# Retention block and SwiGLU feed-forward on one core: the first tile's key rows made on the chip instead of loaded a second time

## The chip, the core and the metric

The kernel runs on one core of a Trainium2 chip. The core has five instruction queues that matter here: TensorE (PE in the profile; its weight loads are listed as PEld), VectorE (DVE), ScalarE (ACT), GpSimd (POOL) and SyncE (SP), which only issues transfers. Each works through its own instructions in order and waits for others by semaphores; transfers (DMA) are carried out by 16 engines that all queues share. The metric is the device time of one execution in microseconds, lower is better; a value given for a kernel is the median of its runs.

## The reference

Eight sequences (batch) of 576 tokens, eight heads of 64 features. Each head has a decay; the scores of queries and keys are weighted by the decay to the power of the distance and summed over the values (no softmax). The result, laid out as 4608 tokens of 512 features, goes through a gated feed-forward layer.

```python
scores = scale * np.matmul(q, k.transpose(0, 1, 3, 2))            # (8, 8, 576, 576), scale = 1/8
gamma = 1.0 - 2.0 ** (-5.0 - np.arange(H))
Dmat = np.where(rel >= 0, gamma[:, None, None] ** rel[None], 0.0)  # rel = query position - key position
attn = np.matmul(scores * Dmat[None], v)
x = attn.transpose(0, 2, 1, 3).reshape(B * S, H * D)               # (4608, 512)
g = x @ w_gate                                                     # 512 x 1536
out = (g * (1.0 / (1.0 + np.exp(-g))) * (x @ w_val)) @ w_out       # (4608, 512), float32
```

## The kernel before

**Pairs.** Attention is done two heads at a time: 8 sequences by 4 pairs of heads make 32 pairs, numbered 0 to 31. A pair's 576 tokens are cut into nine chunks of 64. Within a chunk the scores are computed outright; what earlier chunks add comes through a running state (the decayed sum of key times value). Each pair therefore needs its keys in two layouts: by token (`kn`, tokens on partitions), which together with the values gives the states in `new_states`, and by feature (`kT`, features on partitions, 128 x 576), which together with the queries by feature (`qT`) gives the scores in `scores`.

**Loads.** `load(i)` issues the transfers of pair i, two pairs ahead of its use. Pairs 0 to 3 are special: they are loaded by token and turned by TensorE. From pair 4 on SyncE issues ten transfers a pair (for pairs 4 to 19): `kn` by token (L290, 288 KB), the values `v` by token (L290, 288 KB), then four transfers of 72 KB for the queries and four for the keys (L299). These eight write runs of 32 features, 128 bytes each, into `qk`, so that every 32x32 block of the result lies in `qk` untransposed: partition a*32 + t holds, for quarter a of the pair's features, the tokens j*32 + t. One VectorE transpose of 32x32 blocks over the whole 128 x 576 tile then gives `qT`, a second one `kT` (both L477).

**Buffers.** `qk` has two buffers (pair 11 has a place of its own in `rest`), `kn` three, `v` four; `kT` and the states have one. A load waits until the last reader of the buffer's earlier content is done.

**Ticks.** `tick(t)` advances three pairs by a step. On TensorE: own values of pair t-2 (L517), states of pair t-1 (L528), earlier values of t-2 (L540, L544), scores of t-1 (L552, L558). Behind these, as a list of pieces that are handed to the other engines in turn: ScalarE copies half of the states out of PSUM (`copies`, L569) and scales the keys by token with their decays in place (`keys`, L492), the outputs of pair t-2 go to the tile x of the feed-forward layer (VectorE, or ScalarE for pairs 8 to 19), VectorE masks the scores (L565, L575) and sums the states (L581 to L593), and at the end come the pieces that `transposes(t)` returns for pair t: for pairs 8 to 19 a scaling of the queries on ScalarE (L474), then the two transposes of L477. The next tick's scores need them.

**Tiles.** The feed-forward layer works on tiles of tokens: the first of 512, four more of 1024. The first tile is computed plainly: the up stage multiplies twelve blocks f of 128 hidden features (`up0`, L871, gate into one PSUM bank and value into another, two pairs of banks in turn), ScalarE takes the silu of the gate (L874) and VectorE multiplies it with the value (L875). Then follows the down stage (`down0`, L882). Into these two stages the ticks 4 to 13 are laid by hand: `tick_at` puts ticks 4 to 9 behind blocks f of the up stage and ticks 10 to 13 behind steps of the down stage. The later tiles use schemes with fewer products (L1208 and L1415), with sums on VectorE and GpSimd; pairs 12 to 31 are attended to there.

**Weights.** In the up stage the feed-forward weights are still on their way. `load_w` fetches a raw block (from the sixth on GpSimd issues it) into one of three places; `split` has ScalarE take the wanted bits out of it (L398, L399), and `rounding` has VectorE put them together (L415, L416). `split(j+1)` writes the buffer that `rounding(j-1)` has read, and a raw place is free for the next load when it has been split. In the list of work, silu follows splits on ScalarE, and rounding follows the transposes of the tick before on VectorE.

Of the kernel before, what the change touches and what calls it, by code (L numbers as in the profile page):

```python
# [132 lines left out]
def kernel(  # L133
# [32 lines left out]
    nc = tc.nc  # L166
# [5 lines left out]
    HP = H // 2  # L172
    L = D
    NC = S // L
    NFULL = S // P
    CW = NFULL * P
    SQ = 32
# [59 lines left out]
    def needed(n):  # L237

        last = (min(starts[n] + TW, NT) - 1) // S
        return last * HP + HP - 1 + 3  # L240
# [3 lines left out]
    def whole(i):  # L244

        return HP <= i < needed(2) - 2

    def scaled(i):

        return 0 < i < HP  # L250

    def tokens(src, b, p):
        return src[b, 2 * p : 2 * p + 2].rearrange("h t d -> (h t) d").rearrange("(g p) d -> p g d", p=P)

    def load(i):

        b, p = divmod(i, HP)
        t = kp.tile([P, NC * D], F32, tag="v", name="v", bufs=4)
        late = [rest[:, dn_at + 1280 * (i - 2) + 640 * n :][:, 0 : NC * D] for n in range(2)] if 1 < i < HP else None
        kn = late[1] if late else kp.tile([P, NC * D], F32, tag="kn", name="kn")  # L260
        queue = nc.sync
        if i < HP:
            qk = late[0] if late else ld.tile([P, 2, S // SQ, SQ], F32, tag="qk", name="qk").rearrange("p n j d -> p (n j d)")[:, 0 : NC * D]
            queues = (nc.sync, nc.scalar if i < 2 else nc.sync)
            heads = range(2 * p, 2 * p + 2)
            blocks = lambda a: a[:, 0:CW].rearrange("p (c h d) -> p h c d", h=2, d=D)
            for h, queue in zip(heads, queues):
                if scaled(i):
                    queue.dma_start(out=early[i][:, ts(h % 2, CW // 2)], in_=q[b, h, 0:CW].rearrange("(p c) d -> p (c d)", c=NFULL))
                else:  # L270
                    queue.dma_start(out=blocks(qk)[:, h % 2], in_=q[b, h, 0:CW].rearrange("(c p) d -> p c d", p=P))
            for h, queue in zip(heads, queues):
                queue.dma_start(out=blocks(kn)[:, h % 2], in_=k[b, h, 0:CW].rearrange("(c p) d -> p c d", p=P))
                if i == 0 and queue is nc.sync:
                    nc.sync.dma_start(out=tab[:, 0:NCOL], in_=decays[:, 0:NCOL])

            def values():
                for h in heads:
                    queues[i % 2].dma_start(out=blocks(t)[:, h % 2], in_=v[b, h, 0:CW].rearrange("(c p) d -> p c d", p=P))

            loaded[i] = (qk, kn, t)
            return values
        else:
            if i == needed(1) - 3:
                qk = rest[:, 4096 : 4096 + 2 * S].rearrange("p (n j d) -> p n j d", n=2, d=SQ)
            else:
                qk = ld.tile([P, 2, S // SQ, SQ], F32, tag="qk", name="qk")
            for dst, src in ((kn, k), (t, v)):
                if whole(i):
                    queue.dma_start(out=dst.rearrange("p (g d) -> p g d", d=D), in_=tokens(src, b, p))  # L290
                    continue
                for hl in range(2):
                    queue.dma_start(out=dst[:, 0:CW].rearrange("p (c h d) -> p c h d", h=2, d=D)[:, :, hl, :],
                                    in_=src[b, 2 * p + hl, 0:CW, :].rearrange("(c p) d -> p c d", p=P))
            if not whole(i):
                queue.dma_start(out=t[:, CW : CW + D], in_=v[b, 2 * p : 2 * p + 2, CW:S, :])
            for n, src in enumerate((q, k)):
                for a in range(P // SQ):
                    queue.dma_start(  # L299
                        out=qk[a * SQ : (a + 1) * SQ, n],  # L300
                        in_=src[b, 2 * p + a // 2, :, (a % 2) * SQ : (a % 2 + 1) * SQ].rearrange("(j t) d -> t j d", t=SQ))
        loaded[i] = (qk, kn, t)
# [14 lines left out]
    decays = nc.inline_tensor(table, name="decays").ap()  # L317
    NCOL = 6 * H + 4 * HP + 4 + P
    values = [load(0), load(1)]
    ident = const.tile([P, P], F32, name="ident")  # L320
    make_identity(nc, ident)
    nc.scalar.activation(out=io[:, 0:1], in_=ident[:, 0:1], func=AF.Silu)
    for f in values:
        f()
    load(2)()
    inv, key = tab[:, 0:H], tab[:, H : 2 * H]
    step = tab[:, 2 * H : 2 * H + 2 * HP]
# [25 lines left out]
    for u in range(NF // 2):  # L353
        for gv, w in enumerate((moe_w_gate, moe_w_val)):
            src = w[:, u * 2 * P : (u + 1) * 2 * P].rearrange("(c p) n -> p c n", p=P)
            weights.append((src, [w_up[:, u // 2, gv, 2 * (u % 2) + f].rearrange("p k x -> p (k x)") for f in range(2)]))
    NUP = len(weights)
    for u in range(NF // 2):
        src = moe_w_out[u * 2 * P : (u + 1) * 2 * P, :].rearrange("(f p) n -> p f n", p=P)
# [60 lines left out]
    for m in range(2):  # L420
        load_w(m, (0,))
    load(3)()
    for m in range(2):
        load_w(m, (1,))
# [3 lines left out]
    kT = const.tile([P, S], F32, name="kT")  # L428
# [22 lines left out]
    def light(i):  # L451

        return needed(1) - 6 <= i < needed(2) - 2

    def transposes(i):
        p = i % HP
        qk, kn, vt = loaded.pop(i)
        qT = early[i] if i < HP else qp.tile([P, S], F32, tag="qT", name="qT")
        st[i] = dict(qT=qT, kn=kn, v=vt)
        pieces = []  # L460

        if i < HP:

            for n, (t, src, bank) in enumerate(((kT, kn, bankC), (qT, qk, bankE))):
                for c in range(NFULL):
                    nc.tensor.transpose(bank[:, c : 4 * P : NFULL] if n else bank[:, ts(c, P)], src[:, ts(c, P)], ident)
                pieces.append(lambda t=t, bank=bank: nc.scalar.copy(t[:, 0:CW], bank))
        else:
            if light(i):
                def scale_q():  # L470

                    src = qk[:, 0].rearrange("p (j r) d -> p r j d", r=2)
                    for r in range(2):
                        nc.scalar.activation(out=src[:, r], in_=src[:, r], func=AF.Copy, scale=piece[:, 2 * p + r : 2 * p + r + 1])  # L474
                pieces.append(scale_q)
            for n, t in enumerate((qT, kT)):
                pieces.append(lambda n=n, t=t: nc.vector.transpose(out=t, in_=qk[:, n].rearrange("p j d -> p (j d)")))  # L477

        every = slice(0, P)

        def keys():
            blocks = kn.rearrange("p (g d) -> p g d", d=D)
            if whole(i):
                parts = [(0, every, blocks[:, 0:NFULL]), (1, every, blocks[:, NFULL:NC])]
            else:
                parts = [(hl, every, blocks[:, hl : 2 * NFULL : 2]) for hl in range(2)]
            for hl, rows, at in parts:
                scale = key[rows, 2 * p + hl : 2 * p + hl + 1]
                if 1 < i < HP:
                    nc.gpsimd.tensor_scalar(out=at, in0=at, scalar1=scale, scalar2=None, op0=ALU.mult)  # L490
                else:
                    nc.scalar.activation(out=at, in_=at, func=AF.Copy, scale=scale)  # L492

        if light(i):
            return [lambda: (keys(), pieces[0]())] + pieces[1:]
        return pieces + [keys] if i < HP else [keys] + pieces
# [216 lines left out]
    pieces = []  # L713

    def scale_run(i):
        if scaled(i):
            src = early[i].rearrange("p (h c d) -> p h c d", h=2, d=D)
            dst = loaded[i][0][:, 0:CW].rearrange("p (c h d) -> p h c d", h=2, d=D)
            table = run[:, 8 * i : 8 * i + 8].rearrange("p (h c) -> p h c", h=2).unsqueeze(3).to_broadcast([P, 2, NFULL, D])
            nc.gpsimd.tensor_tensor(out=dst, in0=src, in1=table, op=ALU.mult)  # L720
# [62 lines left out]
    def turn_pair(i):  # L783
        for f in transposes(i):
            f()

    def tick(t, lo=HP, hi=NP, spread=False, then=None):
# [16 lines left out]
        if lo <= t - 1 < hi and whole(t - 2) and not whole(t - 1):  # L804
            decay(slice(0, H), slice(0, H), half[1])
        copies, *masks = masked(t - 1) if lo <= t - 1 < hi else (lambda: None,)
        keys, *new = transposes(t) if lo <= t < hi else (lambda: None,)
        outputs = to_x(t - 2)[0] if lo <= t - 2 < hi else lambda: None
        late = needed(1) - 4 <= t < needed(1) - 2 or light(t - 2)
# [658 lines left out]
    earlier_values(1)  # L1468
    to_x(1)[0]()
    put = transposes(3)  # L1470
    rounding(1, False)
    for f in put:
# [164 lines left out]
```

## Time and profile before

| what | value |
|---|---|
| median of three runs | 1013.4 us (1013.31, 1013.4, 1019.88) |
| profiled execution, its own time | 1012.77 us |
| span of that execution in the profile | 1011.0 us |
| granted TensorE clock | 1.00 throughout |
| packets of SyncE's queue from 39 to 125 us | 46,086, 7.78 MB, 60.0% of the 16 engines' time |
| median time of a 72 KB key load from issue to landing, 39 to 125 us | 5.9 us |
| weight loads by GpSimd, 1024 KB, the same | 7.1 to 9.4 us |

All times inside the profile count from the start of the span. Pairs 4 to 11 are prepared between 45 and 153 us: the first tile's up stage runs until 122.4 us, its down stage until 172.8 us. The prediction shows lines of the page (busy time and share of each engine), of the windows (busy time of each engine in a stretch) and of the timeline (start, duration, engine, line, operation, output<-input with shapes, count; in brackets the time that the engine sat idle before it and who ended that).

### The profile page before, as it was taken

What the parts mean: (1) busy time and instruction counts of PE and PEld (TensorE: products, weight loads), DVE (VectorE), ACT (ScalarE), POOL (GpSimd) and SP (SyncE); (2) the same over time, 40 slices, a digit from 0 to 9 for tenths busy, and PEclk for the clock granted to TensorE, in tenths of its full rate; (3) what the DMA queues carried; (4) which work ended last, traced back from release to release, by engine and by line L of the source; (5) the groups of instructions that cost most, each with busy time, mean ns of one, the idle gap of its engine ahead of it and who ended that gap; (6) DMA issues with size and microseconds to landing.
All of it is one profiled execution on the core that took longest, in us unless ns stands there. A gap on an engine that the chain in (4) does not pass through costs nothing.

```text
span 1011.0 us, 21336 instructions
## 1 busy us (share of the span) xinstructions
PE 1002.8 (99%) x8330; PEld 827.7 (82%) x8330; DVE 717.8 (71%) x1210; ACT 285.7 (28%) x636; POOL 576.3 (57%) x611
## 2 busy tenths in 40 slices
PE   8999999999999999999999999999999999999998
PEld 7645455888888888888888888888888888888887
DVE  5568988678886676977777678866575767566745
ACT  4654622122423321133321202233320012232110
POOL 3511358979587228565565157746672586566614
PEclk9999999999999999999999999999999999999999
DMA  9999977888787886957578786434454454445553
GB/s 228 276 252 281 200 216 260 211 239 217 168 211 235 219 197 218 211 156 198 177 187 222 179 196 202 151 137 155 162 173 141 156 188 146 148 153 185 178 163 103
DMA packets 273932, 194.44 MB, mean 192 GB/s; under 512 B 212328, under 2 KB 241896, under 8 KB 273832
## 3 DMA queue, kind: packets, MB, share of 16 engines
q1 hardware_dynamic: 249448, 99.49, 40.5%
q10 hardware_dynamic: 20208, 79.57, 24.2%
q0 software_dynamic: 4176, 14.03, 4.2%
q8 instruction: 66, 1.08, 0.5%
q14 instruction: 34, 0.28, 0.1%
HBM read 154.11 MB, written 38.93 MB: 191 GB/s over the span
## 4 chain that ended last, share of the span: by engine, by line
PE 91%; SPq 3%; DMA 2%; DVE 1%; issue 1%; ACT 1%; ACTq 0%; DVEq 0%
PE bankB L1208 12%; PE bankE L1208 12%; PE bankA L1208 12%; PE bankC L1208 12%; PE bankE L1415 7%; PE bankC L1415 7%; PE bankB L1415 7%; PE bankA L1415 6%; SPq L299 2%; PE outer L1208 2%; PE inner L1208 2%; PE outer L517 2%; PE outer L544 1%; PE inner L558 1%; PE inner L528 1%
## 5 line engine op out<-in xcount | busy, mean ns | idle before, releaser
L1061 POOL TENSOR_TENSOR rest<-rest 128x512 f32<-128x512 f32 (+1 forms) x143 | 150.7, 1065 | 158.1 <-DVE rest L1061 110.3
L1223 POOL TENSOR_TENSOR arena<-rest,io 128x256 f32<-128x256 f32 x168 | 123.8, 749 | 78.7 <-ACT io L1222 78.1
L1222 ACT ACTIVATE io<-rest 128x256 f32<-128x256 f32 x192 | 79.3, 417 | 209.9 <-DVE rest L1061 139.2
L1208 PE MATMUL bankB<-rest,arena 128*128 128x256 f32 x428 | 110.1, 381 | 0.0
L1208 PE MATMUL bankE<-rest,arena 128*128 128x256 f32 x424 | 107.8, 379 | 0.0
L1061 DVE TENSOR_TENSOR rest<-bankC,rest 128x512 f32<-128x512 f32 x112 | 75.8, 684 | 40.4 <-PE bankC L1208 23.3
L1061 DVE TENSOR_TENSOR rest<-bankB,rest 128x512 f32<-128x512 f32 x110 | 74.8, 685 | 41.5 <-PE bankB L1208 30.4
L1208 PE MATMUL bankA<-rest,arena 128*128 128x256 f32 x408 | 104.0, 379 | 0.0
L1061 DVE TENSOR_TENSOR rest<-bankA,rest 128x512 f32<-128x512 f32 x112 | 75.9, 685 | 38.8 <-PE bankA L1208 20.2
L1061 DVE TENSOR_TENSOR rest<-bankE,rest 128x512 f32<-128x512 f32 x116 | 78.5, 686 | 29.2 <-PE bankE L1208 17.1
L1208 PE MATMUL bankC<-rest,arena 128*128 128x256 f32 x368 | 94.2, 380 | 0.0
L1208 PEld LDWEIGHTS bankB<-rest,arena 128*128 128x128 f32 x428 | 80.7, 190 | 11.9 <-DVE rest L1061 0.9
L1208 PEld LDWEIGHTS bankE<-rest,arena 128*128 128x128 f32 x424 | 80.5, 190 | 11.0
L1208 PEld LDWEIGHTS bankA<-rest,arena 128*128 128x128 f32 x408 | 77.5, 190 | 10.6
L1208 PEld LDWEIGHTS bankC<-rest,arena 128*128 128x128 f32 x368 | 69.4, 190 | 10.0 <-DVE rest L1061 0.6
L1061 POOL TENSOR_TENSOR arena<-arena 128x256 f32<-128x256 f32 (+1 forms) x76 | 70.6, 951 | 8.3 <-PE bankC L1208 7.0
L1415 PE MATMUL bankE<-arena 128*128 128x256 f32 x264 | 61.0, 381 | 0.0
L1415 PE MATMUL bankC<-arena 128*128 128x256 f32 x264 | 60.9, 380 | 0.0
L1415 PEld LDWEIGHTS bankE<-arena 128*128 128x128 f32 x264 | 49.8, 190 | 7.0 <-POOL arena L904 0.2
L1415 PEld LDWEIGHTS bankC<-arena 128*128 128x128 f32 x264 | 49.9, 190 | 6.9
L1415 PE MATMUL bankB<-arena 128*128 128x256 f32 x240 | 55.3, 380 | 0.0
L1415 PE MATMUL bankA<-arena 128*128 128x256 f32 x228 | 52.5, 380 | 0.0
(294 smaller groups left out, 1880.1 us busy)
## 6 DMA issues: line engine op xcount, KB each, us to landing
arena<-up ACTq DMA_DIRECT2D x60, 896.0 KB, 4.8
arena<-dn ACTq DMA_DIRECT2D x60, 384.0 KB, 3.4
arena<-dn SPq DMA_DIRECT2D x44, 384.0 KB, 4.4
out_dram<-rest SPq DMA_DIRECT2D x31, 256.0 KB, 3.5
qk<-in_q_dram SPq DMA_DIRECT2D x108, 72.0 KB, 4.1
qk<-in_k_dram SPq DMA_DIRECT2D x108, 72.0 KB, 3.8
dn<-rest SPq DMA_DIRECT2D x26, 256.0 KB, 3.1
up<-arena SPq DMA_DIRECT2D x13, 512.0 KB, 3.4
```

What stands on the lines that cost most here:

```text
L299: queue.dma_start(out=qk[a * SQ : (a + 1) * SQ, n], in_=src[b, 2 * p + a // 2, :, (a % 2) * SQ : (a % 2 + 1) * SQ].rearrange("(j t) d -> t ...
L517: m = nc.tensor.matmul(value(i, hl, c), s["v"][rows, at], ret[rows, c % 2 if whole(i) else hl, c // 2], start=start, stop=start, skip_grou ...
L528: nc.tensor.matmul(z[half[hl], r, c], s["kn"][chunk(i, hl, 2 * c + r)], s["v"][rows, at], start=True, stop=True, skip_group_check=True)
L544: nc.tensor.matmul(xr[half[hl]] if c + 1 == NC else value(i, hl, c), state[half[hl], c, :], s["qT"][half[hl], ts(c, L)], start=False, stop ...
L558: nc.tensor.matmul(sc[chunk(i, hl, 2 * c + r)[0], r if whole(i) else hl, c], kT[half[hl], at], qT[half[hl], at], start=True, stop=True, sk ...
L1061: eng.tensor_tensor(out=out, in0=a, in1=b, op=ALU.add if sign > 0 else ALU.subtract)
L1208: m = nc.tensor.matmul(b[:, g * TB : (g + 1) * TB], w[:, g], x, start=(opens and g == 0), stop=True, skip_group_check=True)
L1222: nc.scalar.activation(out=s, in_=src[:, 0:TB], func=AF.Silu)
L1223: (nc.vector if busy and o != 2 and qd + 1 < NQ else nc.gpsimd).tensor_tensor(out=hid[:, qd, 2 * H + h, 2 * T + t], in0=src[:, TB : 2 * TB ...
L1415: nc.tensor.matmul(b[:, m * TB : (m + 1) * TB], lhs[:, qd, ts(m, P)], w[:, qd], start=(opens and qd == 0 and m == 0), stop=(qd == NQ - 1), ...
```

## The change

For pairs 4 to 11, those that are turned before the second tile begins, the keys by feature are no longer loaded. VectorE transposes the 32x32 blocks of `kn` (keys by token, before they are scaled) into the half of `qk` in which the loaded keys used to stand. In that form a partition holds 32 features' worth of one of four token groups, with the two heads' and the two halves' blocks interleaved; sixteen ScalarE copies, each of 32 partitions and four or five blocks of 32 elements, put the blocks into the places that they have in `kT`. The query loads, the query transposes and all TensorE work stay. Pairs 12 to 31 keep the loads as they were.

```diff
+    def by_token(i):
+
+        return HP <= i < needed(1) - 2
+
...
-            for n, src in enumerate((q, k)):
+            for n, src in enumerate((q,) if by_token(i) else (q, k)):
                 for a in range(P // SQ):
                     queue.dma_start(
...
-            for n, t in enumerate((qT, kT)):
-                pieces.append(lambda n=n, t=t: nc.vector.transpose(out=t, in_=qk[:, n].rearrange("p j d -> p (j d)")))
+            flat = [qk[:, n].rearrange("p j d -> p (j d)") for n in range(2)]
+            pieces.append(lambda: nc.vector.transpose(out=qT, in_=flat[0]))
+
+            def rows_of_k():
+
+                blocks = flat[1].rearrange("p (g n t) -> p g n t", n=2, t=SQ)
+                to = kT.rearrange("p (c w t) -> p c w t", w=2, t=SQ)
+                for r in range(2):
+                    for hl in range(2):
+                        cs = slice((hl + r) % 2, NC, 2)
+                        gs = slice(hl * (NC // 2 + (1 - r)), hl * (NC // 2 + (1 - r)) + len(range(NC)[cs]))
+                        for w in range(2):
+                            for n in range(2):
+                                nc.scalar.copy(out=to[(2 * hl + n) * SQ : (2 * hl + n + 1) * SQ, cs, w],
+                                               in_=blocks[(2 * r + w) * SQ : (2 * r + w + 1) * SQ, gs, n])
+
+            if by_token(i):
+                nc.vector.transpose(out=flat[1], in_=kn)
+                pieces.append(rows_of_k)
+            else:
+                pieces.append(lambda: nc.vector.transpose(out=kT, in_=flat[1]))
```

`HP` is 4 and `needed(1)` is 14, so `by_token` holds for pairs 4 to 11. The transpose of `kn` is issued when `transposes(t)` is called, ahead of the tick's pieces; the copies are the last of them. In the order of the built program nothing else moves on any engine: VectorE has the same number of transposes, ScalarE has 128 instructions more, and SyncE's queue is 32 transfers shorter.

## The prediction

> **What bounds the kernel now.** I read the share of each engine first, then the windows of the first 180 us (all eight changed pairs lie there), then the places in the TensorE timeline where it sat idle, and from these back along ScalarE and VectorE.
>
> ```profile
> PE 1002.8 (99%) x8330; PEld 827.7 (82%) x8330; DVE 717.8 (71%) x1210; ACT 285.7 (28%) x636; POOL 576.3 (57%) x611
> ```
>
> ```profile
> 39.40:122.40 83.00, 81.17 (x846) 45.25 (x844) 64.09 (x130) 48.07 (x88) 21.55 (x31) 1.00 1.06 241
> 122.40:172.80 50.40, 50.31 (x577) 25.82 (x574) 44.62 (x76) 13.03 (x41) 35.23 (x28) 1.00 0.82 247
> ```
>
> TensorE is busy for 1002.8 of 1011.0 us. The first window is the first tile's up stage with the ticks of pairs 4 to 9, the second its down stage with pairs 10 and 11. After the window's borders and length come the busy us of PE, PEld, DVE, ACT and POOL, then the granted clock (1.00), the DMA share and GB/s. TensorE is idle for 83.00 - 81.17 = 1.83 us in the first window and 0.09 in the second. The DMA share of 1.06 says that the engines which move data have no slack there; ScalarE has 83.00 - 48.07 = 35 us. So nearly all that can be won lies in 1.83 us, two gaps:
>
> ```profile
> 71.47 3.70 PE L871 MATMUL bankA<-rest,arena 128*128 128x512 f32 x8 [0.52 <-ACT io L874]
> 103.74 3.70 PE L871 MATMUL bankA<-rest,arena 128*128 128x512 f32 x8 [1.30 <-ACT io L874]
> ```
>
> The bracket is the idle time before and who ended it: ScalarE's silu, which frees a bank. Why was the silu late? ScalarE works in order, and ahead of each late silu it had stood waiting to split weights (L398):
>
> ```profile
> 67.18 0.69 ACT L398 ACTIVATE rest<-rest 128x512 f32<-128x512 f32 x1 [10.23 <-DVE arena L415]
> ...
> 99.52 0.69 ACT L398 ACTIVATE rest<-rest 128x512 f32<-128x512 f32 x1 [8.51 <-issue]
> ...
> 103.11 0.58 ACT L874 ACTIVATE io<-bankA 128x512 f32<-128x512 f32 x1
> ```
>
> The split overwrites a buffer that VectorE's rounding (L415) reads, and VectorE was held by the transpose of the keys, which waited for their load:
>
> ```profile
> 65.36 0.78 DVE L477 STREAM_TRANSPOSE kT<-qk 128x576 f32<-128x576 f32 x1 [5.03 <-DMA qk<-in_k_dram]
> ...
> 97.44 0.78 DVE L477 STREAM_TRANSPOSE kT<-qk 128x576 f32<-128x576 f32 x1 [3.01 <-DMA qk<-in_k_dram]
> 98.15 0.85 DVE L710 TENSOR_TENSOR x_odd<-outer,tab 128x128 f32<-128x128 f32 x3
> 99.01 0.43 DVE L415 TENSOR_SCALAR arena<-rest 128x512 int32<-128x512 int32 x1
> ```
>
> L415 at 99.01, L398 at 99.52, so the 8.51 us called "issue" are this chain too. The last of a pair's ten loads, the keys by feature, is what holds TensorE.
>
> **What is removed.** For pairs 4 to 11, the four key loads of 72 KB each: 32 issues on SyncE. In its timeline these groups take 7.02, 5.61, 2.13, 4.32, 3.51, 3.48, 2.79 and 2.13 us, 31 us in sum, in which everything behind them in that queue stood: the next pair's loads, the second table (L1485), and from 132.0 us the operand stores (L974). At 128 bytes a packet an issue is 576 packets; the 28 issues from 39 us to 125 us are 16,128 packets. That window's DMA view has 46,086 packets of SyncE's queue taking 60.0% of 16 engines' 86 us, 17.9 ns each; so some 18 us of all engines together are freed (an estimate from that mean). TensorE gains only what ends its two gaps.
>
> Gap one: without the 5.03 us wait VectorE ends pair 5's query transpose at 60.3 us plus the 0.75 of a transpose now ahead of it, has L415 behind it at about 62, and the silu stands at 66 where it stood at 70.83; needed at 70.95. Gone with 5 us to spare. Gap two: the query transpose of pair 7 ended at 94.4 with no wait; plus 0.75, plus L710's 0.85, L415 ends at 96.5. Three splits take 99.52 to 103.11 = 3.6 us in the trace, silu 0.6: ready at 100.7, needed at 102.44 - 0.52 = 101.9. Gone by 1.2 us, if ScalarE is ready to split at 96.5. Gain 1.82 us.
>
> **What is moved.** VectorE keeps two transposes a pair, of one form (128x576, 0.73 to 0.78 us); the keys' is now issued at the head of the tick, from the key tile that was loaded as the pair's first. It therefore delays masks and outputs by 0.75 us and gives that back where the old one stood. The scaling of the keys (L492) now waits for it: at ticks 6 and 7 until 76.0 and 90.3 instead of 74.6 and 88.9, at tick 9 until 126.1 instead of 122.86. Queued behind are only the query scaling and the copies, then splits; TensorE wants tick 9's keys at 129.74 (L528): 0.86 us of scaling fits, cost nothing. The buffer of pair t's queries and keys comes free for pair t+2 when the copies end, no longer with VectorE; copies of pair 6 would end at 80.4, the old transpose ended at 80.7: nothing.
>
> **What is added.** Sixteen ScalarE copies a pair, 32 partitions by 128 or 160 elements (mean 144), SBUF to SBUF, 128 in all. No row has this form. The nearest:
>
> ```profile
> 118.36 0.62 ACT L935 ACTIVATE x_odd<-rest 128x512 f32<-128x512 f32 x1
> 118.88 0.62 ACT L935 ACTIVATE rest<-rest 128x512 f32<-128x512 f32 x1
> ...
> 133.23 0.53 ACT L611 COPY rest<-outer 64x128 f32<-64x128 f32 x2
> 133.67 0.96 ACT L492 ACTIVATE kn<-kn,tab 128x256 f32<-128x256 f32 x2
> ```
>
> L935 is SBUF to SBUF with a constant: 0.62 us long, the next starts 0.52 later. The slope from PSUM copies of 256 and 512 elements (371 and 586 ns) is 0.84 ns an element; 368 fewer make it 0.31 long and 0.21 apart. L611, 64x128 out of PSUM: 133.23 to 133.67 is two, 0.22 apart. Upper bound: L492 and L474, 256 to 320 elements with a scale from a table, 0.43 apart. I take 0.21, since size, source and constant come from the nearest rows: 3.4 us a pair, 27 us in all. Bounds 0.21 and 0.43, with 0.31 where one copy begins only when the last has ended.
>
> [...]
>
> What hides the block: 35 us of idle ScalarE in the first window against five blocks (17 us), and room up to the pair's scores. Each block starts when keys (and from pair 8 the queries) are scaled and must end when TensorE reaches L552 in the next tick:
>
> - pair 4: 46.2 to 53.8; pair 5: 55.7 to 70.0; pair 6: 77.0 to 87.7; pair 7: 91.1 to 112.4; all over 7 us
> - pair 8: 116.8 to 121.7, 4.9 us; pair 9: 127.85 to 131.05, 3.2 us; pair 10: 135.4 to 140.35, 4.95 us; pair 11: 144.7 to 153.1
>
> Pair 9 starts late because VectorE runs without idle from 97.4 us and reaches its key transpose only at 125.3. At 3.4 us only pair 9 is late, by 0.2. For gap two, pair 7's block ends at 94.5 and a split behind it at 95.7, ahead of 96.5.
>
> **Sum**, on the profiled execution (1012.77 us, span 1011.0): -0.52 - 1.30 + 0.2 = -1.6, so 1011.2. The median of the runs shown, 1013.4, is 0.6 above it: 1011.8 us. A measurement of this kernel can tell about 1% from no change, so this is no change in that sense. From 172.8 us on TensorE has no wait for these engines, so the 1.6 us should come through whole.
>
> **Rivals.**
>
> *The gain is given back.* The copies do not overlap: 16 x 0.31 = 5.0 us. Pair 8 then is 0.1 us late, pair 9 1.8, pair 10 0.05; 1.9 against 1.8: 1013.5 us. For: the copies of four ticks carry a wait on their own engine. Against: L398 carries such waits too and keeps 0.57 us between starts at 0.67 length. [...]
>
> *ScalarE sets the end, slower.* At 0.43 the block is 6.9 us and comes after its scores: pair 8 late by 2.0, pair 9 by 3.7 less these 2.0, pair 10 by 1.9, together 5.6; in gap two the split behind pair 7's block starts at 99.2, so 1.30 stays and only 0.52 is won: +5.1, 1018.5 us. It decides from 0.31 a copy on. For: two SBUF rows show 0.43. Against: both have a table operand and up to twice the elements. Over 1% slower would need copies near 0.6 us, which only 512 elements reach here.
>
> *The relief does not reach TensorE.* Splits run earlier but weights are not there: those of gap two were issued by GpSimd at 84.4 and 87.2 and such loads took 7.1 to 9.4 us, so 96.6 against 96.5. If they also are late by the whole 3 us, gap two stays: 1013.1 us. Against: fewer packets in their way.
>
> **How the numbers follow.** Forecast 0.60, given back 0.15, relief not reaching 0.12, slower 0.13. The range runs from 1009.5 (all gained, and up to 2 us between executions) to 1018.5. Faster by over 1% would need 10 us and TensorE idles 8 in all: 0.01. Slower by over 1%: 0.05 of the 0.13, if copies are dearer than any row. Within 1%: 0.94.
>
> **What would show it.** Right: no key wait in VectorE's waits, both L871 gaps under 0.1 us, the new copies 0.20 to 0.25 us apart, L552 of pairs 9 and 10 with under 0.3 us of idle time. Wrong: TensorE waiting for the copies at L552 by over 1 us, a silu still ending a gap near 102 us, or idle TensorE after 173 us.

## The result and the profile after

The changed kernel is slower by half a per cent: 1019.5 us median of 22 runs (1017.73 to 1022.61) against 1013.32 us for the kernel before, run on the same chip. The ratio is 1.0052 with a 95% interval of 1.0038 to 1.0067; that is 5.3 us (3.9 to 6.8), while the two medians lie 6.2 us apart. The forecast was 1011.8 us in a range of 1009.5 to 1018.5. The profiled execution took 1019.25 us, with a span of 1017.6 us and a granted clock of 1.00. Lines have moved in the new file: splits are L402 and L403, roundings L419 and L420, the keys' scaling L515, the transposes L497 (keys) and L481 (queries), the copies L493, states L551, scores L575, up stage L894, silu L897, product L898, down stage L905.

The page's first line after, the busy time of each engine:

```profile
PE 1005.1 (99%) x8330; PEld 828.2 (81%) x8330; DVE 715.2 (70%) x1210; ACT 324.0 (32%) x764; POOL 576.0 (57%) x611
```

ScalarE has the 128 added instructions and 38.3 us more of busy time. The windows of the first tile's up and down stage, with borders where TensorE now begins and ends them:

```profile
39.40:123.85 84.45, 82.11 (x847) 45.74 (x845) 61.77 (x129) 70.09 (x166) 18.97 (x29) 1.00 0.89 221
123.85:178.70 54.85, 51.18 (x574) 26.24 (x574) 43.92 (x77) 29.75 (x93) 39.82 (x32) 1.00 0.63 209
```

TensorE idles 2.34 us in the first (1.83 before) and 3.67 us in the second (0.09 before), while ScalarE is still idle for 14 us of the first and 25 us of the second. The DMA share fell from 1.06 and 0.82 to 0.89 and 0.63. So the transfers went and room in ScalarE was left, as the averages promised, and the time was lost all the same. The timeline of TensorE says where (idle time and its releaser in the bracket):

```profile
104.10 3.70 PE L894 MATMUL bankA<-rest,arena 128*128 128x512 f32 x8 [1.46 <-ACT io L897]
123.11 0.27 PE L575 MATMUL outer<-qT,kT 64*64 64x64 f32 x1 [0.77 <-ACT kT L493]
131.53 0.46 PE L540 MATMUL outer<-ret,v 64*64 64x64 f32 x16 [0.56 <-DVE ret_last L598]
133.56 0.69 PE L551 MATMUL inner<-v,kn 64*64 64x64 f32 x32 [1.57 <-ACT kT L493]
136.41 0.27 PE L575 MATMUL outer<-qT,kT 64*64 64x64 f32 x1 [1.27 <-ACT kT L493]
```

The gap at 71.47 us is gone. The one at 103.74 us (1.30) is still there at 104.10 us (1.46). Four new ones follow, in the ticks of pairs 9 and 10. The next table gives how late TensorE stands: the start of the same instruction after, minus before. A step can be larger than the gaps in the brackets: 1.08 against 0.77 us at the scores of pair 8, 3.99 against 0.56 + 1.57 + 1.27 = 3.40 at those of pair 9. What makes up the rest was not settled.

| at | lag, us | step |
|---|---|---|
| 46 us, ahead of the first changed pair | +0.36 | start-up, differs from run to run |
| behind the scores of pair 4 | +0.79 | +0.43 |
| behind the first gap of before | +0.20 | -0.59 |
| behind the second gap of before | +0.36 | +0.16 |
| behind the scores of pair 8 (down stage starts, 122.39 to 123.83) | +1.44 | +1.08 |
| behind the scores of pair 9 (131.71 to 137.14) | +5.43 | +3.99 |
| behind the scores of pair 10 (141.03 to 146.96) | +5.93 | +0.50 |
| end of the down stage (172.77 to 178.70) | +5.93 | 0 |

Two thirds of it is one tick, that of pair 10, in which the scores of pair 9 are computed. To see what that tick waits for, first ScalarE's timeline around it:

```profile
117.78 5.28 ACT L493 COPY kT<-qk 32x160 f32<-32x160 f32 x16
123.08 0.69 ACT L402 ACTIVATE rest<-rest 128x512 f32<-128x512 f32 x1
123.67 0.66 ACT L403 ACTIVATE rest<-rest 128x512 int32<-128x512 uint32 x1
124.22 0.60 ACT L897 ACTIVATE io<-bankC 128x512 f32<-128x512 f32 x1
...
129.35 0.96 ACT L515 ACTIVATE kn<-kn,tab 128x256 f32<-128x256 f32 x2 [3.24 <-DVE qk L497]
130.22 0.95 ACT L478 ACTIVATE qk<-qk,tab 128x288 f32<-128x288 f32 x2
131.07 5.29 ACT L493 COPY kT<-qk 32x160 f32<-32x160 f32 x16
```

A row of the timeline merges neighbours of one kind: "x16" of 5.28 us is the whole block of a pair, both sizes. VectorE's timeline in the same stretch:

```profile
124.85 0.69 DVE L898 TENSOR_TENSOR arena<-bankE,io 128x512 f32<-128x512 f32 x1 [2.97 <-ACT io L897]
125.46 1.50 DVE L419 TENSOR_SCALAR rest<-rest 128x512 int32<-128x512 int32 x1
127.00 1.64 DVE L420 CUSTOM_DVE_ANT_0 rest<-rest 128x1024 uint16<-128x1024 uint16 x1
128.56 0.77 DVE L497 STREAM_TRANSPOSE qk<-kn 128x576 f32<-128x576 f32 x1
...
132.99 0.48 DVE L616 SCALAR_TENSOR_TENSOR state<-state,tab,inner 128x256 f32<-128x256 f32 x1
```

Read the two as one chain. The copies of pair 8 hold ScalarE from 117.78 to 123.06 us. The last silu of the up stage stands behind them and starts at 124.22. Before, it started at 117.88:

```profile
117.88 0.58 ACT L874 ACTIVATE io<-bankC 128x512 f32<-128x512 f32 x1
```

After, VectorE waits 2.97 us for it with its product. Behind the product in VectorE's queue are the two roundings, and behind these pair 9's key transpose, at 128.56. Now ScalarE waits 3.24 us for that transpose, because the keys may be scaled only after it. Then come two scalings and pair 9's copies, which end at 136.36. The first two scores of pair 9 start at 134.87; the others wait for these copies and start at 136.41. So one block delays the next one by way of the other engine, once round.

VectorE's queue delays TensorE at a second place. The same stretch before, first VectorE, then TensorE:

```profile
122.21 0.68 DVE L875 TENSOR_TENSOR arena<-bankE,io 128x512 f32<-128x512 f32 x1
...
129.07 0.47 DVE L593 SCALAR_TENSOR_TENSOR state<-state,tab,inner 128x256 f32<-128x256 f32 x1
```

```profile
129.74 0.65 PE L528 MATMUL inner<-v,kn 64*64 64x64 f32 x32
```

VectorE's last sum of the states ended at 129.54 us before, and TensorE wrote the next states into the same PSUM place (`inner`) from 129.74 on: 0.2 us of slack. After, the product is 2.64 us later and the sum 3.92, since a longer rounding (1.50 us, 0.89 before) and the transpose now lie between. The sum ends at 133.47 us, and the states start at 133.56. The trace names the copies as releaser of that wait of 1.57 us; by the times it is VectorE.

The copies themselves, as groups by line and shape for the seven pairs that use `qk` (busy us, mean ns of one, idle before):

```profile
L493 ACT COPY kT<-qk 32x160 f32<-32x160 f32 x56 | 17.9, 320 | 1.0
L493 ACT COPY kT<-qk 32x128 f32<-32x128 f32 x56 | 16.5, 295 | 1.2
```

One is 0.31 us long on average, and the block of sixteen takes 5.1 to 5.3 us, 0.32 to 0.33 us from start to start: they don't overlap at all.

### The profile page after: what moved, and what is told of

It is laid out like the page before. It is cut to its first block, busy times and chain, and to the rows that moved or that the text cites. A ratio compares the mean times of both kernels' runs of the same rounds, so it can differ in the third digit from the quotient of the medians.

```text
span 1017.6 us, 21435 instructions
## 1 busy us (share of the span) xinstructions
PE 1005.1 (99%) x8330; PEld 828.2 (81%) x8330; DVE 715.2 (70%) x1210; ACT 324.0 (32%) x764; POOL 576.0 (57%) x611
## 3 DMA queue, kind: packets, MB, share of 16 engines
q1 hardware_dynamic: 230504, 97.13, 38.3%
q8 instruction: 66, 1.08, 0.5%
## 4 chain that ended last, share of the span: by engine, by line
PE 84%; POOL 0%; DVE 0%; ACTq 0%; issue 0%; ACT 0%; DVEq 0%
PE bankB L1231 12%; PE bankE L1231 12%; PE bankA L1231 12%; PE bankC L1231 11%; PE bankE L1438 7%; PE bankC L1438 7%; PE bankB L1438 7%; PE bankA L1438 6%; PE inner L1231 2%; PE outer L1231 2%; PE outer L540 1%; PE outer L567 1%; PE inner L581 1%; PE inner L551 1%; PE bankA L905 1%; PE bankE L905 1%
```

## Experiments

Each is the changed kernel with one edit, but for one which starts from the kernel before. A ratio is to the kernel before, with its 95% interval. "Gaps" are TensorE's waits between 38 and 185 us, read from one profiled execution of each kernel.

**The removal alone.** The key loads go and no copies are added: `kT` is transposed from the query blocks at its old place, so the scores read the queries in the keys' place.

```diff
-                nc.vector.transpose(out=flat[1], in_=kn)
-                pieces.append(rows_of_k)
+                pieces.append(lambda: nc.vector.transpose(out=kT, in_=flat[0]))
```

> Only the removal: pairs 4 to 11 load no keys by feature, no copies are added, and the transpose into kT stands where it stood before and takes the query blocks (the scores of these pairs are thus not those of the reference; the work is the same). This is what the removed loads are worth by themselves. If TensorE's two gaps of 0.52 and 1.30 us come from the wait for these loads, as predicted, both are gone: 1.8 us less than the kernel before, about 1011.5 us. Rival, the relief does not reach TensorE because weights or ScalarE are late anyway: at least the 1.30 us stays, 1012.8 us or more.

Measured: 1012.15 us, ratio 0.9981 (0.9963 to 0.9998), 1.9 us less (0.2 to 3.7), and no gap at all. This is the term of the prediction that held: taking the loads away removes both waits, and the gain agrees with the 1.82 us that TensorE idled there, though the interval is wide.

**A quarter of the copies.** Four copies of 128 partitions in place of sixteen of 32. The rows land in other places than the scores need; the key transpose stays where the change put it.

```diff
-                for r in range(2):
...
+                for hl in range(2):
+                    cs = slice(hl, NC, 2)
+                    gs = slice(hl * (NC // 2 + 1), hl * (NC // 2 + 1) + len(range(NC)[cs]))
+                    for n in range(2):
+                        nc.scalar.copy(out=to[:, cs, n], in_=blocks[:, gs, n])
```

> The changed kernel with four copies a pair in place of sixteen, each over all 128 partitions without moving between them (the keys' places are then wrong). The transposes, waits and removed loads are those of the changed kernel. Theory A, the length of the block in ScalarE's order makes the loss: the block is 1.3 us in place of 5.3, all waits of TensorE for kT go, and the removed loads show: 1011.5 to 1012.5. Theory B, the moved transpose makes it (the scaling of the keys waits for a late VectorE, 10.5 us in sum and 3.2 at pair 9, and states and scores behind it): the waits at pair 9 stay for the most part: 1015 to 1016.

Measured: 1012.58 us, ratio 0.9985 (0.9970 to 1.0000), no gap, close to the 1011.5 to 1012.5 of theory A. ScalarE's timeline and the groups:

```profile
49.02 0.93 ACT L491 COPY kT<-qk 128x160 f32<-128x160 f32 x4
```

```profile
L491 ACT COPY kT<-qk 128x160 f32<-128x160 f32 x14 | 3.8, 315 | 0.0
L491 ACT COPY kT<-qk 128x128 f32<-128x128 f32 x14 | 3.5, 295 | 0.0
```

With a short block the later place of the transpose costs nothing that can be measured. And a copy of 128 partitions is as long as one of 32 (0.305 us on average), but the next starts 0.21 us after it: four take 0.93 us from the first start to the last end, that is (0.93 - 0.31) / 3. That is the spacing that the prediction took from rows of 128 partitions. The overlap of two neighbours is 0.31 - 0.21 = 0.10 us, as much as L935 shows before (0.62 - 0.52). The changed kernel's copies of 32 partitions, 0.32 to 0.33 from start to start, do not have it.

**Sixteen copies that stay on their partitions.** The same number and size, with input and output on the same 32 partitions (again other places than the scores need).

```diff
-nc.scalar.copy(out=to[(2 * hl + n) * SQ : (2 * hl + n + 1) * SQ, cs, w],
+nc.scalar.copy(out=to[(2 * r + w) * SQ : (2 * r + w + 1) * SQ, cs, n],
```

> The changed kernel's sixteen copies a pair of 32 partitions, but each writes the partitions that it reads (the keys' places are then wrong). It asks why a copy in the changed kernel takes 0.33 us of the queue when the four copies over 128 partitions of the run before stood 0.21 apart at the same length (0.295 and 0.315 us). Theory P1, moving from one group of partitions to another is what stops neighbours from overlapping: 0.21 apart, a block of 3.4 us, and by the prediction's sum some 1012 us. Theory P2, a part of the partitions is enough: 0.33 apart, 5.3 us, and the time of the changed kernel, 1018.5 to 1019.5.

```profile
48.83 4.32 ACT L493 COPY kT<-qk 32x160 f32<-32x160 f32 x16
...
128.35 0.69 PE L551 MATMUL inner<-v,kn 64*64 64x64 f32 x32 [0.60 <-ACT kT L493]
130.24 0.27 PE L575 MATMUL outer<-qT,kT 64*64 64x64 f32 x1 [0.31 <-ACT kT L493]
```

A length of 0.305 us again, a block of 4.32 us: 0.27 from start to start. So neither idea about the spacing was right alone. Of the 0.12 us between 0.21 and 0.33, one half goes with 32 partitions, the other with moving to different ones. (The four wide copies also are fewer in a row and take other blocks, which was not varied by itself.) Measured: 1014.71 us, ratio 1.0009 (0.9997 to 1.0020), between the two theories: one microsecond off each block takes away 4 of the 5 us of loss.

**Pairs 4 to 7 alone, and pairs 8 to 11 alone.** The bounds of `by_token` are changed, nothing else.

```diff
-        return HP <= i < needed(1) - 2
+        return HP <= i < 2 * HP                  # pairs 4 to 7
+        return 2 * HP <= i < needed(1) - 2       # pairs 8 to 11
```

> The change for pairs 4 to 7 alone; 8 to 11 load their keys as before. In the trace of the changed kernel TensorE lost nothing net up to the tick of pair 8 (its position against the kernel before stayed at +0.35 us) and 5.6 us at the ticks of pairs 9 to 11. If the loss is local to the ticks in which ScalarE and VectorE are dense (theory: the block of copies comes too late for the scores of pairs 8 to 10), this is within 1 us of the kernel before, 1012.5 to 1014. Rival, the loss is built up by all blocks together (ScalarE falls behind from the first on): half of the loss, 1016.

> The change for pairs 8 to 11 alone. If the loss is local to these ticks: all of it or a little more, since the two gaps of the kernel before stay too: 5 to 6 us over the kernel before, 1018.5 to 1019.5. Rival, built up by all blocks: half, 1016.

Measured: 1016.76 us, 1.0035 (1.0017 to 1.0053), and 1016.24 us, 1.0021 (1.0002 to 1.0040). These are the times of the rival, half of the loss each. TensorE's timeline of the first, then that of the second:

```profile
103.84 3.70 PE L894 MATMUL bankA<-rest,arena 128*128 128x512 f32 x8 [1.55 <-ACT io L897]
...
132.42 0.70 PE L551 MATMUL inner<-v,kn 64*64 64x64 f32 x32 [1.57 <-issue]
```

```profile
128.02 0.46 PE L540 MATMUL outer<-ret,v 64*64 64x64 f32 x16 [0.47 <-DVE ret_last L598]
130.06 1.14 PE L551 MATMUL inner<-v,kn 64*64 64x64 f32 x32 [1.58 <-ACT kT L493]
```

Pairs 8 to 11 had been expected to carry nearly all of the loss and carry some 2 us of it. In the first kernel pairs 8 to 11 have no copies, and the states of tick 10 still wait: VectorE's last sum (L616) ends at 132.32 us there and the states start at 132.42. VectorE is late there because ScalarE waited for late loads of `w_out` (4.4 us in three waits between 100 and 134 us). So the loss is not local to a pair: lateness is handed on. That it travels by splits, loads and roundings is read from this one trace. The second kernel keeps the chain of pairs 8 and 9 whole (its waits for the silu and the transpose are 2.98 and 3.25 us), but arrives without the two old gaps in its profiled execution, though pairs 4 to 7 still load their keys and ScalarE's splits wait 7.93 and 8.11 us, until 64.95 and 82.50 us, for VectorE's roundings in the ticks of pairs 5 and 6. The old gaps are thus not the same in every run. The states' row of 1.14 us, 0.70 in the other kernel, shows something else: behind that wait the rows are longer than in the other kernel up to the last scores at 133.08 us (0.80 us, 0.67 there), and the granted clock from 122 to 180 us was 0.97, where it was 1.00 in the other kernel and in the kernel before. Here it cost little, since the copies ended only at 132.86 us.

**The key transpose earlier.** All eight pairs and all sixteen copies, but from pair 6 on VectorE turns the keys ahead of the rounding that stands before the tick (in the down stage ahead of `down0`), instead of at the head of the tick. `turn_early`, whose definition the diff below leaves out, issues this transpose.

```diff
+        if f in tick_at and f > 3:
+            plan.append(lambda t=tick_at[f]: turn_early(t))
         round_until({4: 12, 6: 13, 8: 14, 9: 15, 10: 16, 11: 17}.get(f, f + 2))
...
+        if m in tick_at and tick_at[m] < FIRST:
+            turn_early(tick_at[m])
         down0(f)
```

> The changed kernel with VectorE's transpose of the key tile issued earlier for pairs 6 to 11: ahead of the rounding before the tick (ahead of the step of the down stage for 10 and 11). The copies stay as they are. Theory A, the length of the block alone makes the loss: 1 us back at most, 1018 to 1019. Theory B, VectorE's order matters too: at pair 9 ScalarE no longer waits 3.2 us for that transpose, so the scores' wait at the next tick (1.27 us and more) goes, and VectorE's masks stand 0.75 us earlier: 2 to 2.5 us back, 1016.5 to 1017.5.

Measured: 1014.03 us, ratio 1.0001 (0.9985 to 1.0016). The loss against the kernel before is gone, not only the 2 to 2.5 us expected. ScalarE's, TensorE's and VectorE's timelines:

```profile
124.02 5.29 ACT L502 COPY kT<-qk 32x160 f32<-32x160 f32 x16
```

```profile
129.21 0.69 PE L560 MATMUL inner<-v,kn 64*64 64x64 f32 x32 [0.44 <-ACT kT L502]
```

```profile
128.63 0.48 DVE L625 SCALAR_TENSOR_TENSOR state<-state,tab,inner 128x256 f32<-128x256 f32 x1
```

The copies are as slow as in the changed kernel (5.1 to 5.29 us), but pair 9's start at 124.02 us instead of 131.07. The gap near 104 us is gone too: pair 7's block starts at 90.93 instead of 93.80 us, and the silu behind it at 100.61 instead of 103.48. What remains is 0.44 us at the states, which start 0.10 us after VectorE's last sum has ended (129.11), and 0.18 us at the scores of pair 10.

Together with the quarter of copies this shows the cause. The clearest measure is the stretch that the change touches: from the first block of 256-column products in the up stage to the first product of the second tile, 39.38 to 172.77 us or 133.39 us before. It leaves out the start-up, which ends between 39.36 and 40.65 us in the profiled executions. One profiled execution each:

| kernel | block of copies | key transpose | stretch against before, us |
|---|---|---|---|
| removal alone | none | at its old place, from the queries | -2.15 |
| a quarter of the copies | 0.93 us | late | -2.16 |
| the key transpose earlier | 5.1 to 5.3 us | early | -0.53 |
| changed kernel | 5.1 to 5.3 us | late | +5.58 |

Measured from the removal alone, the late transpose costs nothing where the block is short, the long block costs 1.6 us where the transpose is early, and both together cost 7.7 us. The two halves, pairs 4 to 7 and pairs 8 to 11, stand at +2.78 and +2.55 in the same measure, about half of the 5.58 each.

**The other way to the first gain.** The kernel before, all loads kept; the key transposes of pairs 5, 6 and 7 are issued behind the roundings that follow (four in the trace), so that a late load holds none of these up. The diff leaves out where they are issued, and that the loads of pair 9 move behind pair 7's transpose.

```diff
-                pieces.append(lambda n=n, t=t: nc.vector.transpose(...))
+                turn = lambda n=n, t=t: nc.vector.transpose(...)
+                if n and i in (5, 6, 7):
+                    put_off.append(turn)
+                else:
+                    pieces.append(turn)
```

> The kernel before with all its loads, no copies; only the transposes into kT of pairs 5, 6 and 7 are issued later, behind the next two roundings (the load of pair 9 moves behind pair 7's). If the two gaps of the kernel before come from VectorE standing at these transposes until the key loads land, both go without any load removed: 1011.5 to 1012.5 us. If the traffic itself (weights late) makes them: 1013 to 1014.

Measured: 1013.84 us, 1.0004 (0.9992 to 1.0017), no change. VectorE's waits between 38 and 185 us, and a row of TensorE's timeline:

```profile
DVE qT L479 <- DMA qk<-in_q_dram: 4.9, 1, 4.9
DVE kT L479 <- DMA qk<-in_k_dram: 4.8, 2, 4.2
```

```profile
129.40 0.69 PE L534 MATMUL inner<-v,kn 64*64 64x64 f32 x32 [0.76 <-issue]
```

Both old gaps are gone here, but not the waits for loads: one key wait of 4.2 us stays and one of 4.9 us for a query load is new. A late key transpose held up the scores for 0.52 us, and the states of tick 10 start 0.76 us late, 0.09 us after VectorE's last sum. So the stretch is 0.42 us shorter than before instead of 1.8, and none of that is left in the measured time.

**Half of the copies on GpSimd.**

```diff
+                                if r:
+                                    nc.gpsimd.tensor_copy(out=at, in_=of)
+                                else:
+                                    nc.scalar.copy(out=at, in_=of)
```

> The changed kernel with eight of a pair's sixteen copies on GpSimd, which is idle for most of the up stage. ScalarE's block is then 2.6 us. Theory A (length of ScalarE's block): the waits at pairs 8 to 10 go for the most part, 1012.5 to 1014 us. Against it: from pair 9 on GpSimd has sums of its own (1.4 us each) ahead of these copies, and copies there may cost more than the 0.40 us that its 128x256 copy takes in the kernel before; then the scores wait for GpSimd: 1016 or more.

```profile
55.87 0.27 PE L578 MATMUL outer<-qT,kT 64*64 64x64 f32 x1 [1.80 <-POOL kT L495]
...
56.59 5.40 PE L897 MATMUL bankA<-rest,arena 128*128 128x512 f32 x8
```

Measured: 1018.63 us, ratio 1.0055 (1.0042 to 1.0069), the "1016 or more" of the expectation. Eight copies take GpSimd 2.8 us for most pairs, 0.36 from start to start, no quicker than ScalarE (0.33). But they stand behind its own work, the issuing of transfers: in the first tick 1.79 and 0.72 us of issues stand right ahead of them, they end at 55.81 us, and TensorE waits 1.80 us for them. The eight products behind that wait take 5.40 us in place of 3.70, the next eight 3.60; the granted clock of this execution was 0.998 in the mean (1.00 in the changed kernel's). So with 1.70 us more behind it the wait cost almost twice its length in this execution. Near 194, 200 and 223 us TensorE waits 0.3 to 0.6 us for sums that GpSimd makes later. Up to the second tile the stretch is 1.8 us longer than before; the rest of the loss comes behind it and was not followed up.

**A smaller change that keeps the gain?** The early transpose with copies for pairs 4 to 7, and for pairs 5 and 7 alone, whose key loads ended the two old gaps.

```diff
-        return HP <= i < needed(1) - 2
+        return HP <= i < 2 * HP      # pairs 4 to 7
+        return i in (5, 7)           # pairs 5 and 7
```

> Pairs 4 to 7 get the copies, key transposes of pairs 6 and 7 early. Against the run of pairs 4 to 7 with the transposes at the head of the tick (1.0035) it tells what the early transpose is worth without pairs 8 to 11. If the late transpose of pair 7 made the splits and with them the later weight loads late: 0.998 to 1.000, with no gap near 104 and 132 us. If the block itself delays the splits: still 1.002 to 1.0035, with the 1.5 us gaps near 104 and 132 us.

> Only pairs 5 and 7, whose key loads ended TensorE's two gaps in the kernel before, get the copies; the key transpose of pair 7 is issued ahead of the rounding before its tick, as in the run with early transposes. If the loss comes from the blocks of the later pairs and from late transposes alone, both gaps go and nothing comes in their place: 0.998 to 0.999 of the kernel before, 1011.3 to 1012.3 us. If each block of 5.3 us costs by delaying the splits behind it, or if the key loads of pair 6, which stay, become the late ones, nothing is left of the gain or it turns: 1.000 to 1.002.

Measured: 1.0011 (0.9998 to 1.0025; 1014.62 us) and 0.9994 (0.9981 to 1.0007; 1012.91 us), each between the two cases of its expectation. In the first the gap near 104 us is gone, and one of 1.57 us at 130.67 us, in front of the states of tick 10, is left. The second has no gap, and its stretch is 1.87 us shorter than before, so the whole of the first gain is there at the second tile. But TensorE then idles 0.87 us at 272.87 us, where the kernel before idles nothing. So no version with all the key rows in their places is measurably faster than the kernel before.

## Why the prediction was wrong

The forecast was 1.6 us less than before on the profiled execution; 5.3 us more were measured. Point by point, in the order of its sum:

- **The removal: right.** -1.82 us was said, -1.9 us (-3.7 to -0.2) measured for the removal alone; no key-load wait is left in VectorE.
- **The copies' price: mis-sized.** 0.21 us apart was taken, 0.33 measured. The length was right (0.31 said, 0.295 and 0.320 measured), the overlap was not. It came from L935, 128 partitions wide, and such copies do come 0.21 apart; those of 32 partitions that change their place, 0.33 apart at a length of 0.31, don't overlap. The second row that seemed to support it was misread: two copies of L611 in 0.53 us with a length of 0.26 each are 0.27 apart and don't overlap either. The 0.22 came from dividing by two a distance that ends with another instruction, L492. By its own bounds ("0.31 where one copy begins only when the last has ended") the price stood at the rival "the gain is given back", whose block of 16 x 0.31 = 5.0 us was near the 5.1 to 5.3 measured and whose 1013.5 us still is far below the measured time. The rival at 0.43 us a copy gave 1018.5 us; that is close to what was measured, but by a price that no copy had, so by luck.
- **Where a block starts: mis-timed.** The wait of the scaling for VectorE's transpose was counted at ticks 6, 7 and 9, but with VectorE's times of the trace before, and at the other ticks not at all. Pair 4's block was to start at 46.2 us and started at 49.19, pair 7's at 91.1 and at 93.80. With 5.1 us more and four splits of 1.14 us behind it, the silu comes at 103.48 us, later than before. So gap two stayed, by the mechanism that the 0.43 rival had for it, only at a lower price.
- **"0.86 us of scaling fits, cost nothing": the step that failed.** The scaling itself is not what TensorE waited for: at tick 9 it ended at 130.31 us, VectorE's last sum at 133.47. "Queued behind are only the query scaling and the copies, then splits" is what was wrong. Behind the copies in ScalarE's queue stands also the silu of the last up block, and behind that VectorE's product, its roundings and the next pair's transpose, which releases the next scaling. The prediction costed each pair's block against the start times of the trace before, as if they stayed; in fact block and transpose form a loop over two engines, and the delay of one tick is the starting point of the next. Tick 10, where this arrives, is +3.99 us, where 0.2 us was forecast and 1.8 by the rival with almost the same price of a copy. So the price alone does not explain the loss, and with the early transpose the same price costs 1.6 us in place of 7.7.
- **The other user of VectorE.** That TensorE's states overwrite what VectorE's last sum reads, with 0.2 us of slack before, was in the trace (129.54 and 129.74 us) and not counted. It ended 1.57 us of TensorE's idle time.
- **"The 1.6 us should come through whole" from 172.8 us on: not so in every run.** Six profiled kernels reach the second tile with a shorter stretch than before: the removal alone, the quarter of copies, the copies that stay on their partitions, the early transpose with eight and with two pairs, and the late key transposes. All six idle 0.9 to 1.8 us between 185 and 290 us, nearly all of it near 272 us, where before idled nothing; the kernels with a longer stretch do not idle near 272 us. From the second tile to the end the six take 1.6 to 2.5 us longer than before. GpSimd's sums end close by, but what decides it was not settled.

What stays open besides: the end is 6.6 us later in the profiled pair where 5.93 are accounted for up to 178.70 us, and 0.36 of these lie ahead of the first changed pair.

## What to carry to other kernels

Before calling an added block on an idle engine hidden, follow its queue one full turn: what stands behind the block, which engine waits for that, and whether that engine's next instruction releases the following block. When an edit turns "load, then transpose" into "transpose, then scale, then copy", the transpose has become the head of a chain and should be issued as early as its input allows; here its place alone took the ratio from 1.0052 to 1.0001. Price a small operation by a row with the same number of partitions and the same move between partitions, not only with the same size. And read a gain at the end of the run as well as where it arises: the two pairs with early copies won 1.87 us up to the second tile and kept no measurable part of it.

## What the runs showed of the hardware

ScalarE copies from SBUF to SBUF of 128 and 160 elements were 0.293 to 0.295 and 0.315 to 0.320 us long whether over 32 or 128 partitions, but the distance from one to the next was 0.21 us over 128 partitions, 0.27 over 32 in place, and 0.33 over 32 that move to other partitions. On GpSimd the same small copies took 0.315 and 0.319 us and came 0.36 apart (the seven pairs that use `qk`, pair 4's first block aside). Why the distance follows the partitions was not tried.

Behind two waits of TensorE the products that followed were longer too. Behind the 1.80 us in the run with half of the copies on GpSimd eight products took 5.40 us in place of 3.70, with a granted clock of 0.998 over that execution. Behind the 1.58 us in the run of pairs 8 to 11 the row of states took 1.14 us in place of 0.70, with a granted clock of 0.97 from 122 to 180 us (1.00 before). Behind the 1.57 us at 133.56 us in the changed kernel the same row took 0.69 us and the clock stayed at 1.00; what decides this was not tried.
